# Expert weights at the end of a Fourier and expert kernel: six conversions moved, six loads placed elsewhere, fewer fill matmuls

## The chip, the cores and the metric

One core of one Trainium2 chip runs the whole program. The metric is device microseconds of one execution, and less is better. The core has five engines that run side by side, each in the order of its own queue: TensorE (PE, matmuls; its weight loads stand apart as PEld), VectorE (DVE), ScalarE (ACT), GpSimd (POOL) and SyncE (SP, which here only starts DMAs). POOL starts the gathers, whose row addresses come from memory.

## The reference, cut to what matters

```python
def _attn_ref(x, w_r, w_i, b_r, b_i):           # x: 8 x 2496 x 256
    X = np.fft.rfft(x, axis=1)
    Yr = Xr @ w_r - Xi @ w_i + b_r
    Yi = Xr @ w_i + Xi @ w_r + b_i
    Yr, Yi = soft_threshold(Yr, 0.01), soft_threshold(Yi, 0.01)
    return np.fft.irfft(Yr + 1j * Yi, n=2496, axis=1)

def _moe_ref(x, w_gate, w1, w2, capacity):      # x: 19968 x 256, 8 experts, capacity 80
    expert_idx, gate_w = argmax and its softmax of x @ w_gate
    for e in range(8):
        tok_idx = the 80 tokens of expert e with the largest gate_w
        h = np.maximum(x[tok_idx] @ w1[e], 0.0)           # w1[e]: 256 x 1024
        out[tok_idx] = gate_w[tok_idx, None] * (h @ w2[e])  # w2[e]: 1024 x 256
    return out                                  # all other rows are zero
```

## The kernel before, in words

The transform of length 2496 is split as 39 by 64 and done with matmuls, one batch after the other, in two halves each. The last step of the inverse transform is not done for all tokens. Its input lies in a DRAM tensor (`hd`), and for a chosen token 13 of its rows of 256 numbers are gathered and added with 13 weights (`wv`). The gate's values are formed for all tokens, and VectorE picks the best 80 of each expert by rounds of maximum and replace (`level1`, `level2`, `merge`, `choose`). This chooses 640 tokens. 128 of them are known early and gathered first (`ahead_`, `scaleA`, `columnsA`); the other 512 come as four groups of 128, numbered g = 0 to 3.

For each group `begin` and `feedY` issue on POOL a gather of ids (`tok`, L1124), then one of seven rows of `hd` (`hx`), one of the weights (`wv`) and one of the other six rows (`hx`). `position` adds the rows up on ACT, DVE and POOL (L1178, L1179, L1186, L1201, L1206, L1209, L1213). For groups 0 and 1 PE adds some of them with diagonal matrices that DVE makes (L1176, L1240). `columnsY` brings the sum onto PE, and ACT and DVE write it as an fp16 pair into `xT` (L1256, L1258). Then `experts` runs, expert by expert, `ffn1` (L1271, followed by L1273 on ACT and L1275 on DVE into `hp`) and `ffn2` (L1287, followed by L1290, L1291 or L1293 on ACT into `wt`), and `give` transposes finished groups (L1297), scales them (L1299) and scatters them into the output (L1300). Experts 0, 1 and part of 2 need group 0; expert 4 needs group 2; expert 6 needs group 3.

Expert weights arrive as fp32 and are used as a pair: a high half in fp16, made by ACT (a "conversion", L852, L855 or L858), and the rest in bf16, which is the fp32 weights less the high half (a "subtraction", on DVE at L860 or on POOL at L867). The text calls a quarter of an expert's weights (e, k, i): expert e, k = 0 for w1 and 1 for w2, half i. Each is 128 partitions by 1024 numbers, 512 KB. `prepW` makes these steps and `doW` traces the next of them. `slots["pairN"]` is the region of expert N: 4096 fp32 columns that hold, in this order, the high half of w1, the high half of w2, the rest of w1, the rest of w2, 1024 columns each. Before a quarter is converted it must be loaded into a free place: experts 4 to 6 are loaded into the region of expert 7 and into `stage`, and expert 7 into the region of expert 0, once that expert has been computed. Quarters (6,1,0) and (6,1,1) go into the first two pieces of expert 7's region, which (5,1,0) and (5,1,1) leave once DVE has subtracted them. The loads after these two are those of expert 7, and all six stand at L835 in SP's queue.

The order of each engine's queue is chosen at build time by a list scheduler that takes what is ready, in the order of tracing. `tc.issue_after(i)` puts what is traced in it behind instruction i on the same engine. `behind(key)` does so for an instruction that was noted in `ev`, and does nothing where the key is not there yet. In `ev`, ("A", "ra", e) and ("A", "rv", e) are L1273 and L1275 of expert e, ("A", "xa", g) and ("A", "xv", g) are L1256 and L1258 of group g. `exps` holds the exponentials of the gate (L785), `dev` and `d2s` evictions at L560 and L594, `sums` the three additions of `combine` on POOL (L579 to L581), `egs` the last gather of `ahead_`, `ffs` the copy of a flag on DVE (L1071), `hbs` and `hops` earlier DMAs on SP. `BUSY` counts matmuls without use that keep PE at work: the first number is that of L1768, the second that of L1226 after `columnsA`; four more of L1226 stand in the middle of group 0's columns.

Of the kernel before, what the change touches and what calls it, by code (L numbers as in the profile page):

```python
# [141 lines left out]
def fourier_mix_then_moe(ctx, tc, x, w_r, w_i, b_r, b_i, wg, w1, w2, t1, t2, vq, v3, v0, v1f, vt, sg, cst, cb, out):  # L142
# [276 lines left out]
    mids = []  # L419
    hbm = []  # L420
# [398 lines left out]
    def prepW(e, pool, name):  # L819
# [3 lines left out]
        def load(k, i):  # L823
            if (k, i) in got:
                return
            if e < E - 1:
                wt = stage2[0][:, i] if (e, k) == (2, 1) and stage2 else stage[(0, 1, 4, 5)[2 * k + i]] if e == 6 else stage.pop(0)
                if e != 6 and not ((e, k) == (2, 1) and stage2):
                    stage.append(wt)
            else:  # L830
                wt = slots["pair0"][:, 1024 * (2 * k + i):1024 * (2 * k + i) + 1024]
            w = w2[e].rearrange("(c p) d -> p c d", p=128)[:, 4 * i:4 * i + 4] if k else w1[e].rearrange("(c p) f -> p c f", p=128)[:, i:i + 1]
            if 4 * e + 2 * k + i >= 26 and after:
                with tc.issue_after(hbs[-1].ins if e == 6 else hops[-1].ins):
                    nc.sync.dma_start(wt.rearrange("p (c f) -> p c f", c=1 + 3 * k), w)  # L835
            else:
                (nc.sync.dma_start if e >= WS or stage2 else wdma)(wt.rearrange("p (c f) -> p c f", c=1 + 3 * k), w)
            got[k, i] = wt

        def step(k, i):  # L840
# [9 lines left out]
            if e == 7 and after:  # L850
                with behind(("A", "xa", 4) if k + i == 2 and ("A", "xa", 4) in ev else ("A", "ra", (3, 4)[k])):
                    nc.scalar.activation(wh[:, c:c + 1024], wt, AF.Copy)  # L852
            elif e >= HX and after:
                with behind(("A", "ra", k)) if e == 6 else tc.issue_after(dev[-1].ins):
                    nc.scalar.activation(wh[:, c:c + 1024], wt, AF.Copy)  # L855
            else:
                with tc.issue_after((exps[-2], exps[-2], d2s[0], exps[-1])[2 * k + i].ins) if after else ExitStack():
                    nc.scalar.activation(wh[:, c:c + 1024], wt, AF.Copy)  # L858
            if (e, k, i) in WV:
                sub = lambda: nc.vector.tensor_tensor(wl[:, c:c + 1024], wt, wh[:, c:c + 1024], op=ALU.subtract)  # L860
                with (behind(("A", 'xv', 3)) if e == 7 else behind(("A", "rv", k)) if e == 6 else tc.issue_after(ffs[-1].ins)) if after else tc.issue_after(sels[-1].ins):
                    sub()
            else:

                def sub():
                    with tc.issue_after((egs if (e, k, i) > (5, 0, 0) else sums)[-1].ins) if sums and e > 4 else ExitStack():
                        nc.gpsimd.tensor_tensor(wl[:, c:c + 1024], wt, wh[:, c:c + 1024], op=ALU.subtract)  # L867
                held.append(sub) if hold else sub()
# [293 lines left out]
    def position(S, nm, g, wv, hx):  # L1162
# [3 lines left out]
        if g in PEQ:  # L1166
# [12 lines left out]
            nc.scalar.activation(z, hx[1], AF.Copy, scale=w(1))  # L1179
# [49 lines left out]
    BUSY = (6, 12)  # L1229
# [89 lines left out]
    def ahead_():  # L1319
# [9 lines left out]
        with tc.issue_after(sums[-1].ins):  # L1329
            get(NL)  # L1330
            gather(hA[:, :1792], hd[0][:5 * 192], ct[:, NL, 1:2])
            gather(wv, vt, ct[:, NL, 2:3])
            egs.append(gather(hA[:, 1792:3328], hd[1][:5 * 192], ct[:, NL, 1:2]))
# [60 lines left out]
    def experts(S, n, gate, sid):  # L1394
# [27 lines left out]
        feedY(S)  # L1422
        feedY(S)
        first(0)
        if after:
            doW(2)
# [366 lines left out]
    with tc.high_priority():  # L1793
# [10 lines left out]
        S0.update(ct=sA["ct"])  # L1804
        sA.update(rest=S0["rest"])
    doW(len(wq) - 8)
    for q in wq[:4]:
        q[2]()
# [49 lines left out]
```

## Time and profile before

| what | us |
|---|---|
| three runs | 573.61, 1066.68, 579.05 |
| median of the three | 579.05 |
| the profiled execution's own time | 574.14 |
| its span, from the first to the last instruction | 572.4 |
| PE busy in it | 525.7 |

The profile's times count from the first instruction. The span covers the program's instructions, and 1.74 us of the profiled execution's own time lie around it. The transform takes the first 480 us, in which PE is nearly always busy. The work that the change touches lies after that: the picking of tokens to 508 us, the gathers and the experts from 512 to 564 us, and the last scatter, which starts at 564.49 us.

### The profile page before, as it was taken

The numbers are of one execution on the slowest core, as the hardware profiler recorded it, in microseconds if no ns is written. First come the engines' busy times: TensorE is split into PE (matmuls) and PEld (weight loads), VectorE is DVE, ScalarE is ACT, GpSimd is POOL, SyncE is SP. The second block draws the span as 40 slices with busy tenths as digits, with TensorE's granted clock in tenths as the row PEclk, the third lists the DMA queues.
The fourth block names the chain that finished last, engine by engine and source line by source line (L and its number), as shares of the span: only waits on it lengthen the run. The fifth ranks groups of instructions, "written<-read, shape, count | busy, mean of one in ns | idle before, by whom it ended". The sixth has DMA issues, their size and how long they took to land. (4 is left out here: it accounts for less than half of the span.)

```text
span 572.4 us, 12944 instructions
## 1 busy us (share of the span) xinstructions
PE 525.7 (92%) x5067; PEld 383.6 (67%) x5067; DVE 386.5 (68%) x741; ACT 328.1 (57%) x479; POOL 371.0 (65%) x295
## 2 busy tenths in 40 slices
PE   8869999999999999999999999979799998888993
PEld 3355676667677867786687768756676785556983
DVE  4423555666767676766766976784999958876950
ACT  2325768575756665675667565654564635641861
POOL 4105887686866786767678677576993166856661
PEclk9979999999999999999999999999999977989997
DMA  6898898987999798978996897889882778579800
GB/s 221 267 250 233 298 216 279 264 256 226 265 286 298 218 268 257 299 187 254 279 318 186 229 260 211 258 256 290 238 261 78 209 215 281 165 247 394 302 31 25
DMA packets 97224, 137.03 MB, mean 239 GB/s; under 512 B 26600, under 2 KB 77808, under 8 KB 95402
## 3 DMA queue, kind: packets, MB, share of 16 engines
q1 hardware_dynamic: 91115, 118.10, 71.1%
q0 software_dynamic: 2624, 11.45, 5.6%
q10 hardware_dynamic: 3418, 6.58, 3.6%
q8 instruction: 42, 0.69, 0.5%
q14 instruction: 25, 0.20, 0.1%
HBM read 70.82 MB, written 65.29 MB: 238 GB/s over the span
## 5 line engine op out<-in xcount | busy, mean ns | idle before, releaser
L450 PE MATMUL ps<-XT,WM 128*128 128x288 f16 (+4 forms) x1536 | 217.4, 298 | 7.5 <-DVE Gs L568 2.1
L450 PEld LDWEIGHTS <-WM 128*128 128x128 f16 x1536 | 149.4, 98 | 65.3 <-issue 7.5
L479 DVE SCALAR_TENSOR_TENSOR R<-ps,thr,tp 128x674 f32<-128x674 f32 (+1 forms) x56 | 48.6, 867 | 78.8 <-ACT tp L474 75.0
L497 POOL TENSOR_TENSOR YT<-R,YT 128x1408 f16<-128x1408 f32 (+1 forms) x28 | 73.5, 2623 | 31.9 <-ACT YT L496 30.2
L474 ACT ACTIVATE tp<-ps,thr 128x674 f32<-128x674 f32 (+1 forms) x56 | 43.6, 778 | 82.9 <-PE ps L450 78.0
L482 POOL TENSOR_TENSOR R<-R,sgs 128x576 f32<-128x576 f32 x28 | 36.5, 1302 | 75.0 <-DVE R L479 75.0
L301 POOL TENSOR_TENSOR xs<-xt,xs 117x1024 f16<-117x1024 f32 (+1 forms) x39 | 76.3, 1957 | 9.9 <-ACT xs L300 9.8
L386 PE MATMUL ps<-t2s,z 128*128 128x128 f16 x320 | 57.8, 222 | 9.0 <-DMA z<-zs 7.2
L337 DVE TENSOR_TENSOR zs<-ps,zs 128x1024 f16<-128x1024 f32 (+1 forms) x45 | 51.1, 1136 | 18.0 <-ACT zs L336 17.6
L392 DVE TENSOR_TENSOR XT<-ps,XT 128x640 f16<-128x640 f32 (+2 forms) x64 | 51.6, 815 | 15.6 <-ACT XT L391 15.0
L391 ACT ACTIVATE XT<-ps 128x640 f16<-128x640 f32 (+2 forms) x64 | 44.5, 701 | 24.2 <-PE ps L388 20.5
L387 PE MATMUL ps<-t2s,z 128*128 128x128 f16 x320 | 57.8, 222 | 0.0
L388 PE MATMUL ps<-t2s,z 128*128 128x128 f16 x320 | 57.8, 221 | 0.0
L315 PE MATMUL ps<-xs,t1s 117*128 117x512 f16 x213 | 52.5, 379 | 1.0 <-POOL xs L301 0.8
L336 ACT ACTIVATE zs<-ps 128x1024 f16<-128x1024 f32 (+1 forms) x45 | 43.0, 955 | 11.8 <-PE ps L315 6.9
L565 DVE TENSOR_TENSOR YO<-ps,YO 128x768 f16<-128x768 f32 (+1 forms) x50 | 45.3, 907 | 6.0 <-ACT YO L564 6.0
L616 PE MATMUL ps<-YO,vqs 128*128 128x512 f16 (+1 forms) x252 | 48.0, 330 | 1.5 <-DVE hs L623 1.5
L496 ACT ACTIVATE YT<-R 128x1408 f16<-128x1408 f32 (+1 forms) x28 | 35.5, 1267 | 21.2 <-POOL R L493 21.1
L553 PE MATMUL ps<-wgi,YT 128*128 128x144 f16 (+1 forms) x302 | 43.2, 228 | 3.3 <-DVE R L479 1.9
L554 PE MATMUL ps<-wgi,YT 128*128 128x136 f16 (+1 forms) x302 | 42.5, 225 | 0.0
L564 ACT ACTIVATE YO<-ps 128x768 f16<-128x768 f32 (+1 forms) x50 | 38.5, 775 | 3.9 <-PE ps L554 1.7
L616 PEld LDWEIGHTS <-vqs 128*128 128x128 f16 x252 | 24.3, 98 | 23.2 <-issue 2.5
(330 smaller groups left out, 978.6 us busy)
## 6 DMA issues: line engine op xcount, KB each, us to landing
out<-zero SPq DMA_DIRECT2D x48, 384.0 KB
z<-zs SPq DMA_DIRECT2D x35, 512.0 KB
hd<-hs SPq DMA_DIRECT2D x90, 192.0 KB
xt<-in_x SPq DMA_DIRECT2D x41, 312.0 KB
z<-z SPq DMA_DIRECT2D x14, 528.0 KB
pair<-in_moe_w SPq DMA_DIRECT2D x14, 512.0 KB
z<-z SPq DMA_DIRECT2D x14, 432.0 KB
wt<-in_moe_w ACTq DMA_DIRECT2D x10, 512.0 KB
```

The costliest lines, as they stand in the source:

```text
L301: nc.gpsimd.tensor_tensor(xs[:, 1, :ng], xt[:, j0:j0 + ng], xs[:, 0, :ng], op=ALU.subtract)
L315: nc.tensor.matmul(pt[:, 512 * j:512 * j + 512], t1s[:, t], xs[:, h, 2 * j:2 * j + 2], start=(i == 0), stop=(i == 2))
L337: evD.append(nc.vector.tensor_tensor(zs[:, :ng, 1, :], pv[:, :ng], zs[:, :ng, 0, :], op=ALU.subtract))
L386: nc.tensor.matmul(o, zz(0), t2s[:, cl, 0, :], start=True, stop=False)
L387: nc.tensor.matmul(o, zz(0), t2s[:, cl, 1, :], start=False, stop=False)
L388: nc.tensor.matmul(o, zz(1), t2s[:, cl, 0, :], start=False, stop=True)
L392: nc.vector.tensor_tensor(ov(1), pv, ov(0), op=ALU.subtract)
L450: nc.tensor.matmul(pt[:, o:o + e - a], WM[:, dh, m, wh, 128 * eh:128 * eh + 128], XT[:, dh, xh, c, a:e], start=(i == 0), stop=(i == len(te ...
L479: nc.vector.scalar_tensor_tensor(fv(Rf), pv, thr[:, eh, ri, 1:2], fv(t), op0=ALU.add, op1=ALU.min)
L497: nc.gpsimd.tensor_tensor(yv(1), rv, yv(0), op=ALU.subtract)
L565: dvs.append(nc.vector.tensor_tensor(yol, yy, yoh, op=ALU.subtract))
L616: nc.tensor.matmul(o, tab[:, v], yo(h), start=(i == 0), stop=(i == 2))
```

## The change

- Loads: quarters (6,1,0) and (6,1,1) go into the region of expert 0, into the places of w1's high half and w1's rest. (7,0,0) and (7,0,1) go into the fourth and the second piece of expert 7's own region, (7,1,0) and (7,1,1) into the places of w2's high half and rest in the region of expert 0. The six loads are put behind each other on SP. The first four are traced behind `ffn1` of expert 0; before, expert 6's were traced ahead of `experts` and expert 7's at expert 6.
- Conversions: (4,1,1) stands behind the eviction `d2s[0]` where it stood behind the last exponential; (5,0,0) behind the last exponential where it stood behind the last eviction; (6,0,0) and (6,0,1) behind L1179 of group 0 where they stood behind L1273 of expert 0; (7,0,0) and (7,0,1) behind L1256 of group 2 where they stood behind L1273 of expert 3.
- Subtractions: on POOL (5,0,0) stands behind nothing where it stood behind `combine`, and (5,0,1) behind the first gather of `ahead_` where it stood behind its last. On DVE (5,1,0) and (5,1,1) stand behind a new copy of one column that reads the ids of group 1, so it waits for that gather; (6,0,0) and (6,0,1) are traced ahead of `ffn1` of expert 0, so the key that held them behind L1275 is not there.
- Fill: `BUSY` is (4, 4) where it was (6, 12).

```diff
+    got1 = []
+    loads = []
...
-            if e < E - 1:
+            if after and e > 5 and e + k > 6:
+                wt = slots["pair7"][:, 3072 - 2048 * i:4096 - 2048 * i] if e + k == 7 and not k else slots["pair0"][:, 1024 * (e - 6) + 2048 * i:1024 * (e - 5) + 2048 * i]
+            elif e < E - 1:
...
-                wt = slots["pair0"][:, 1024 * (2 * k + i):1024 * (2 * k + i) + 1024]
+                wt = slots["pair0"][:, 1024 * (k + 2 * i):1024 * (k + 2 * i) + 1024]
...
             if 4 * e + 2 * k + i >= 26 and after:
-                with tc.issue_after(hbs[-1].ins if e == 6 else hops[-1].ins):
-                    nc.sync.dma_start(wt.rearrange("p (c f) -> p c f", c=1 + 3 * k), w)
+                with tc.issue_after(loads[-1].ins) if loads else ExitStack():
+                    i_ = nc.sync.dma_start(wt.rearrange("p (c f) -> p c f", c=1 + 3 * k), w)
+                loads.append(i_)
...
             if e == 7 and after:
-                with behind(("A", "xa", 4) if k + i == 2 and ("A", "xa", 4) in ev else ("A", "ra", (3, 4)[k])):
+                with behind(("A", "ra", 4) if k else ("A", "xa", 2)):
...
             elif e >= HX and after:
-                with behind(("A", "ra", k)) if e == 6 else tc.issue_after(dev[-1].ins):
+                with behind(("A", "ra", 1) if k else ("A", "az", 0)) if e == 6 else tc.issue_after((dev if k + i else exps)[-1].ins):
...
-                with tc.issue_after((exps[-2], exps[-2], d2s[0], exps[-1])[2 * k + i].ins) if after else ExitStack():
+                with tc.issue_after((exps[-2], exps[-2], d2s[0], d2s[0])[2 * k + i].ins) if after else ExitStack():
...
-                with (behind(("A", 'xv', 3)) if e == 7 else behind(("A", "rv", k)) if e == 6 else tc.issue_after(ffs[-1].ins)) if after else tc.issue_after(sels[-1].ins):
+                with (behind(("A", 'xv', 3)) if e == 7 else behind(("A", "rv", k)) if e == 6 else tc.issue_after(got1[-1].ins)) if after else tc.issue_after(sels[-1].ins):
...
-                    with tc.issue_after((egs if (e, k, i) > (5, 0, 0) else sums)[-1].ins) if sums and e > 4 else ExitStack():
+                    with tc.issue_after(egs[0 if e == 5 else -1].ins) if egs and after and (e, k, i) > (5, 0, 0) else ExitStack():
...
-            nc.scalar.activation(z, hx[1], AF.Copy, scale=w(1))
+            ev[nm, "az", g] = nc.scalar.activation(z, hx[1], AF.Copy, scale=w(1))
...
-    BUSY = (6, 12)
+    BUSY = (4, 4)
...
-            get(NL)
+            egs.append(get(NL))
...
         feedY(S)
+        if after:
+            doW(2)
         feedY(S)
         first(0)
         if after:
-            doW(2)
+            for q in wq[:4]:
+                q[2]()
...
+        with tc.issue_after(ffs[-1].ins):
+            got1.append(nc.vector.tensor_copy(sp.tile([128, 1], F32, name="t1"), ctA[:, 1, 0:1]))
...
-    for q in wq[:4]:
+    for q in wq[:2]:
         q[2]()
```

## Rows read from the trace of the kernel before

**Rows 1.** The head of the page: span and instructions.

```profile
span 572.4 us, 12944 instructions
```

**Rows 2.** The chain that ended last, in order of time: start us, us, what.

```profile
519.11 5.88 DMA wv<-in_vt,tok
...
526.81 2.61 PE pf L1271 x46
```

**Rows 3.** Windows: busy us of each engine (instructions), granted clock, DMA share, GB/s.

```profile
502.50:510.50 8.00, 6.00 (x22) 2.79 (x21) 6.02 (x23) 5.25 (x12) 4.05 (x3) 0.79 1.00 384
...
514.00:526.00 12.00, 9.86 (x67) 7.13 (x67) 5.46 (x14) 2.10 (x6) 8.93 (x9) 1.00 1.03 373
...
528.00:530.00 2.00, 2.00 (x25) 2.00 (x23) 1.97 (x6) 0.91 (x3) 1.14 (x2) 0.50 0.99 345
```

**Rows 4.** DMA queues and issues, 512 to 520 us; an issue's last number: us to landing.

```profile
q1 hardware_dynamic: 1045, 1.04, 47.7%
...
hx<-hd,tok POOLq DMA_INDIRECT x3, 6.9
```

**Rows 5.** DMA queues, 512 to 543 us: packets, MB, share of 16 engines.

```profile
q1 hardware_dynamic: 2400, 3.15, 30.9%
q0 software_dynamic: 1344, 6.85, 57.6%
```

**Rows 6.** Timeline of SP, weight loads: start us, us over all, what, how many.

```profile
513.02 1.50 SPq L835 DMA_DIRECT2D pair<-in_moe_w  x2
...
529.39 6.16 SPq L835 DMA_DIRECT2D pair<-in_moe_w  x4
```

**Rows 7.** Timeline of POOL: start us, us, what, count, idle before and its end.

```profile
486.17 2.14 POOL L867 TENSOR_TENSOR pair<-pair,pair 128x1024 bf16<-128x1024 f32 x1 [4.34 <-ACT pair L858]
...
502.50 2.15 POOL L867 TENSOR_TENSOR pair<-wt,pair 128x1024 bf16<-128x1024 f32 x1
...
512.52 1.28 POOL L1124 DMA_INDIRECT hx<-hd,tok  x1 [2.37 <-ACT pair L1338]
...
515.36 0.94 POOL L1124 DMA_INDIRECT hx<-hd,tok  x1 [0.31 <-issue]
...
543.81 4.23 POOL L867 TENSOR_TENSOR pair<-pair,pair 128x1024 bf16<-128x1024 f32 x2
```

**Rows 8.** Timeline of DVE.

```profile
502.71 2.00 DVE L1049 TENSOR_TENSOR Gs<-gh,t0b 8x48 f32<-8x48 f32 x1
...
505.37 0.20 DVE L1050 TENSOR_TENSOR Gs<-pfn,pfb 8x48 f32<-8x48 f32 x1
...
511.76 2.36 DVE L860 TENSOR_TENSOR pair<-pair,pair 128x1024 bf16<-128x1024 f32 x2
519.88 0.76 DVE L1176 TENSOR_TENSOR wt<-ident,wv 128x128 f32<-128x128 f32 x2 [5.76 <-issue]
...
530.88 2.36 DVE L860 TENSOR_TENSOR pair<-pair,pair 128x1024 bf16<-128x1024 f32 x2 [0.36 <-ACT pair L855]
```

**Rows 9.** Timeline of ACT.

```profile
506.41 5.51 ACT L1338 ACTIVATE pair<-pair 128x256 f32<-128x256 f32 x13 [0.88 <-DMA pair<-in_vt,tok]
...
525.07 0.51 ACT L1178 ACTIVATE y<-hx,wv 128x256 f32<-128x256 f32 x1 [4.01 <-DMA wv<-in_vt,tok]
...
536.37 2.01 ACT L855 ACTIVATE pair<-pair 128x1024 f16<-128x1024 f32 x2
...
542.68 2.00 ACT L852 ACTIVATE pair<-pair 128x1024 f16<-128x1024 f32 x2
...
549.04 1.99 ACT L852 ACTIVATE pair<-pair 128x1024 f16<-128x1024 f32 x2
```

**Rows 10.** Timeline of PE.

```profile
517.27 2.75 PE L1226 MATMUL pf<-pair 128*128 128x512 f16 x12
...
535.43 1.89 PE L1271 MATMUL pf<-xT,pair2a 128*128 128x80 f16 x48
...
545.27 0.44 PE L1297 MATMUL ps<-ident,wt 128*128 128x128 f32 x2 [1.00 <-ACT wt L1290]
```

## The prediction

> **What bounds the kernel now.** I read the page first, then the chain that ended last, then windows over the end of the span, and then the timelines of the five engines there. The change is traced behind the transform, so only the last 90 us of the span [rows 1] can move. The chain shows the reader a single transfer on the path to the first expert: the gather of group 1's weights `wv`, issued at 519.11 and 5.88 us on its way. After it come one step each on ACT and DVE and then PE's first `ffn1`, the bulk of which starts at 526.81 [rows 2]. The windows say why the transfer is slow: from 514 to 526 us the DMA engines are full (share 1.03, 373 GB/s) [rows 3]. The queue view says with what: to 520 us 1.04 MB are weights on SP's queue [rows 4], and from 512 to 543 us it is 3.15 MB of weights beside 6.85 MB of gathers [rows 5]. The weights of that early stretch are SP's two loads from 513.02; the other four start at 529.39 [rows 6]. So the stretch from 512 to 526 us waits for DMA, and two loads that nobody needs before 536.37 [rows 9] stand in it. From 526 us on PE is nearly always at work, with short waits for ACT, such as the 1.00 us at 545.27 [rows 10].
>
> **The early moves (480 to 512 us).** The subtraction of (4,1,1) goes into POOL's 4.34 us of idle time ahead of 486.17, and (5,0,0) takes its old place [rows 7]. Their conversions swap places on ACT in the same way. Price 0: POOL is idle there, and if that cover were gone 2.14 us would fall on `combine`. (5,0,1) leaves 502.50 [rows 7] for the place that (5,0,0) had. That frees DVE: L1049, an addition of 48 columns, took 2.00 us and ended with POOL's 2.15 us subtraction, where a like one, L1050, took 0.20 [rows 8]. So DVE's picking of tokens ends 1.8 us sooner. I let only 0.2 of it through, because what comes next is held by others: the DMA engines are full until 510.50 (share 1.00) [rows 3], the first `hx` gather must wait for the stores in that stretch, and ACT scales the early rows until 511.92 (506.41 and 5.51) [rows 9]. The gather starts at 512.52 [rows 7]. Bounds: 0 and -1.8; I take **-0.2**, nearer the rows that hold it. The Trainium skill, SBUF — State Buffer, section "Who interferes with whom", says that a VectorE instruction with two SBUF inputs and a GpSimd instruction that reads SBUF exclude each other for a whole instruction. The pair 502.50 and 502.71 agrees, and the same rule would spare the gathers from the DVE subtractions that the change puts beside them, since it takes descriptor writing to need another port. By the rule alone the +0.4 below would be 0 and the sum -2.5.
>
> **The two loads.** Without 1.04 MB ahead of or between the gathers, at 373 GB/s [rows 3, 4], group 0's second `hx` and group 1's `wv` land up to 1.04/0.373 = 2.8 us sooner. The least is 0, if POOL's issuing sets the pace: a gather's issue takes 0.94 us [rows 7], and four make a group. Issuing is a little faster than the DMA engines (a group is a quarter of 6.85 MB, 1.71 MB, 4.6 us at 373 GB/s, against some 5 us for four issues with the pauses of 0.31 between them, [rows 3, 5, 7]), so the two are close, and part of the gain must be lost to POOL. I take **-2.4**.
>
> **Quarters (6,0,0) and (6,0,1).** Their conversions (2 us by the like pair at 536.37) fall into ACT's wait of 4.01 us ahead of 525.07 [rows 9]: price 0, and if `wv` landed at once they would cost up to 2. Their DVE subtractions (2.36 us at 530.88 [rows 8]) now stand among group 0's and group 1's additions. DVE does the same work in all, so what they cost early comes back at 530.88. What does not come back is a delay of the gathers: beside L860 at 511.76 [rows 8] the `hx` issue took 1.28, and 0.94 at 515.36 [rows 7], so 0.34 for each that meets one. Bounds 0 and +2.36; I take **+0.4**, one such meeting. The new copy of ids holds (5,1,0) and (5,1,1) behind the ids' landing. DVE is idle for 5.76 us behind them, ahead of 519.88 [rows 8], so the price is 0, and up to 2 if group 0's rows came that early.
>
> **Fill.** Twelve matmuls at 517.27 take 2.75 us [rows 10]; four take 0.9. PE waits for `wv` of group 0 behind them, so alone this is worth 0; once that lands sooner, the twelve would have held group 0's columns, which is why both edits belong together. Two fewer of L1768 also go to PE idle time. What can be lost is the clock, priced below as a rival.
>
> **Loads of (6,1,0) and (6,1,1) later.** They now wait for the end of `ffn1` of expert 0, as two of expert 7's did at 529.39 [rows 6]. With the 2.2 gained so far that is about 527.2. The trace gives no landing for SP's loads, so I take the nearest, 6.9 us for `hx` in a full stretch [rows 4]: 534.1. Their conversions start at 536.37 [rows 9], less 2.2, at 534.2. So the cover is just used up: behind the conversions on ACT stand L1273 of the next experts, for which `ffn2` waits. Bounds 0 and +2; I take **+0.3**.
>
> **Conversions of (7,0,0) and (7,0,1).** At 542.68 they hold ACT for 2.00 us [rows 9], and L1290 and group 2's L1256 stand behind them; PE waits 1.00 for L1290 [rows 10]. Behind L1256 of group 2 they hold neither. Bounds 0 and -1.00; I take **-0.9**.
>
> **A new wait.** (7,1,0) is converted into the second piece of expert 7's region, from which (7,0,1) is now subtracted by POOL. The conversions of (7,1,*) start at 549.04 [rows 9] and POOL's two subtractions run from 543.81 for 4.23 us [rows 7], to 548.04. That is 1.0 us of margin. With the first pair's conversions 2 us later relative to the rest, the margin is -1. Behind this ACT instruction stand L1290 of expert 3 and L1273 of expert 5, and PE waits for both. Bounds 0 (the scheduler puts other work ahead) and +2.1 (one more subtraction); I take **+0.7**.
>
> **The sum.** -0.2 - 2.4 + 0.4 + 0.3 - 0.9 + 0.7 = -2.1. The profiled execution took 574.14 us, 572.4 of it span [rows 1], so 572.0. That execution is 4.91 below the median shown, 579.05, and 0.53 above the lowest run. I forecast on its footing and let the range reach up for the other.
>
> **The rivals.** *No gain*: POOL's issuing sets the gathers' pace, or PE's clock takes the gain. In the profile the clock is granted at 0.50 (1.2 GHz) from 528 to 530 us, after PE's short stretches of work to 526 [rows 3], and 46 matmuls took 2.61 us where 48 took 1.89 at full clock [rows 2, 10], some 0.8 us for each such stretch. With eight fewer matmuls the clock could fall twice, +1.6, and with the two loads worth 1.2 rather than 2.4 the sum is -2.1 + 1.6 + 1.2 = +0.7: 574.8. The Trainium skill, TensorE: Matmul & The Clock Gate, section "What's actually happening", takes the slow clock as the default that activity lifts. By that rule less fill is a loss, and this rival is where it would show. *Slower*: ACT's wait at the conversion of (7,1,0). If the two loads bring nothing (0 for -2.4), that wait costs one whole subtraction, 2.1 for the 0.7: -2.1 + 2.4 + 1.4 = +1.7: 575.8. It decides once POOL ends (7,0,1) later than ACT reaches the conversion by more than the 1.0 that the earlier edit saves. *More gain*: the loads bring 2.8, ACT's wait goes whole, no new wait comes, and the slow clock at 528 vanishes (0.8): -0.2 - 2.8 - 1.0 - 0.8 = -4.8: 569.3. *The change does not do what it says*: the scheduler takes the old order on ACT and DVE, and only the loads' places change, which is the first rival's time.
>
> **How the numbers follow.** Forecast 572.0 with chance 0.45, its own range 570 to 574; no gain 0.22; slower 0.18; more gain 0.12; 0.03 for what none of these covers. The low end goes below the third rival by 1.8, to 567.5. The high end takes the slower rival with most of the 4.91 by which the median lies above the profiled execution: 575.8 + 4.2 = 580. Faster or slower by over 2% is 11.5 us, about what a measurement of this kernel can tell from no change, and no term or sum of terms reaches it: faster 0.04, slower 0.04, within 0.92.
>
> **What would show it.** Right: `wv` of group 1 lands near 522.6 and PE's first `ffn1` runs at about 524.5; L1049 takes 0.2; no 1.00 wait at L1297 behind L1290. Wrong: conversions L855 of (6,1,*) that wait for a DMA, a conversion L852 that waits for POOL's L867 with PE idle behind it, or a granted clock of 0.50 over more than the 3 us of now.

## The result and the profile after

The median of 20 executions after the change is 578.43 us, that of 20 before it 575.45 us. The ratio is 1.0062, with an interval of 1.0037 to 1.0087: some 3.5 us slower, where 2.1 us faster was forecast. (All ratios are taken from the fast executions of both kernels alone, so they are not quite the ratios of the medians.) A second measurement of the same kernel in a later session (`after_anchor` below) gave the same median, 578.45, beside 577.83 for before: 1.0015 [0.9982, 1.0047]. The two together put the cost at about 0.4%, 2.2 us. The first interval says 2.1 to 5.0 us slower, the second 1.0 faster to 2.7 slower. By 2% this is no change; the sign of the sum was wrong all the same, and that is what had to be explained.

The profiled execution after took 581.63 us, high among its own 20 (576.35 to 586.23). So its rows show what can happen, and prices are taken from several kernels' traces. The head of its page, for [rows 1]:

```profile
span 579.8 us, 12925 instructions
```

The chain that ended last (start us, us, what), for [rows 2]:

```profile
506.79 9.35 DMA pair<-hd,tok
...
516.16 1.31 ACT pair L1343 x3
...
521.38 5.22 DMA hx<-hd,tok
...
532.96 1.80 PE pf L1276 x46
534.77 10.69 DMA pair<-in_moe_w
545.48 1.06 ACT pair L860
546.57 1.23 DVE pair L865
547.79 0.40 DVE yp L1218
548.19 0.40 DVE hp L1280
548.60 0.04 issue
548.64 1.76 PE pf L1276 x24
```

Two transfers stand here that the chain before did not show. One is the gather of the early rows (`pair<-hd,tok`), for whose rows ACT, POOL and so the first `hx` gather wait. It is not new: the chain before is followed back only to 514.11, and before, too, the first `hx` gather waited 2.37 us for ACT's work on these rows [rows 7]. The other is new: a weight load of 10.69 us, for which ACT, DVE and PE wait in turn. It is the one that the prediction had costed with 6.9 us. Timelines of SP, ACT and PE (idle before, and its end, in brackets) for [rows 6, 9, 10]:

```profile
534.77 8.16 SPq L839 DMA_DIRECT2D pair<-in_moe_w  x6
...
525.54 1.99 ACT L860 ACTIVATE pair<-pair 128x1024 f16<-128x1024 f32 x2
530.12 0.51 ACT L1183 ACTIVATE y<-hx,wv 128x256 f32<-128x256 f32 x1 [2.59 <-DMA wv<-in_vt,tok]
...
545.48 1.06 ACT L860 ACTIVATE pair<-pair 128x1024 f16<-128x1024 f32 x1 [4.44 <-DMA pair<-in_moe_w]
...
548.64 1.76 PE L1276 MATMUL pf<-xT,pair 128*128 128x80 f16 x24 [3.28 <-DVE hp L1280]
```

The conversion of (6,1,0) at 545.48 waits 4.44 us for its load, and PE then waits 3.28. The conversions of (6,0,*) at 525.54 do fit into ACT's wait for `wv`. Timelines of POOL and DVE, for [rows 7, 8]:

```profile
498.85 1.06 POOL L1129 DMA_INDIRECT tok<-cid,posA  x1 [0.17 <-DVE ps L922]
499.93 2.14 POOL L872 TENSOR_TENSOR pair<-wt,pair 128x1024 bf16<-128x1024 f32 x1
504.25 0.97 POOL L1129 DMA_INDIRECT pair<-hd,tok  x1 [2.18 <-issue]
...
517.82 2.00 POOL L1129 DMA_INDIRECT hx<-hd,tok  x1 [6.22 <-ACT pair L1343]
...
529.44 1.61 POOL L1129 DMA_INDIRECT hx<-hd,tok  x1 [0.30 <-issue]
531.36 1.30 POOL L1129 DMA_INDIRECT wv<-in_vt,tok  x1 [0.30 <-issue]
...
505.94 0.20 DVE L1054 TENSOR_TENSOR Gs<-gh,t0b 8x48 f32<-8x48 f32 x1
```

The addition that had taken 2.00 us takes 0.20, as forecast. But the gather of the early rows at 504.25 comes 5.40 us after the gather of their ids at 498.85. The same two gathers before:

```profile
495.63 1.06 POOL L1124 DMA_INDIRECT tok<-cid,posA  x1 [0.17 <-DVE ps L917]
496.71 2.14 POOL L867 TENSOR_TENSOR pair<-wt,pair 128x1024 bf16<-128x1024 f32 x1
499.01 0.97 POOL L1124 DMA_INDIRECT pair<-hd,tok  x1 [0.16 <-issue]
```

There it was 3.38. Windows of after (busy us of PE, PEld, DVE, ACT, POOL; clock, DMA share, GB/s), for [rows 3]:

```profile
514.00:526.00 12.00, 9.65 (x60) 8.26 (x58) 4.01 (x8) 5.86 (x15) 6.65 (x6) 0.86 0.59 200
526.00:538.00 12.00, 9.79 (x125) 8.84 (x126) 10.77 (x25) 4.56 (x12) 9.50 (x9) 0.86 0.88 294
538.00:548.00 10.00, 6.62 (x180) 6.39 (x178) 5.25 (x14) 5.56 (x16) 3.52 (x5) 1.00 1.02 380
```

From 514 to 526 us the DMA engines are no longer full (share 0.59; 1.03 before), in part because the gathers start at 517.82 only. From 538 to 548 us, where the late loads run beside the last groups' gathers, they are full (1.02), and PE is busy for 6.62 of 10 us.

### The profile page after: what moved, and what is told of

Read it like the earlier page. It is cut to its first block, busy times and chain, and to the rows that moved or that the text cites. A ratio compares the mean times of both kernels' runs of the same rounds, so it can differ in the third digit from the quotient of the medians.

```text
span 579.8 us, 12925 instructions
## 1 busy us (share of the span) xinstructions
PE 529.1 (91%) x5057; PEld 389.5 (67%) x5057; DVE 385.0 (66%) x742; ACT 328.5 (57%) x479; POOL 372.7 (64%) x295
## 4 chain that ended last, share of the span: by engine, by line
PE 48%; DVE 15%; DMA 13%; POOL 7%; ACT 7%; issue 7%; SPq 2%; POOLq 0%; ACTq 0%; DVEq 0%
PE ps L452 21%; PE ps L315 6%; PE ps L618 4%; DMA wt<-in_moe_w 3%; DMA xt<-in_x 3%; DVE R L481 2%; DMA pair<-in_moe_w 2%; PE ps L555 2%; PE ps L556 2%; ACT tp L476 2%; DMA z<-zs 2%; DMA pair<-hd,tok 2%; POOL R L484 2%; PE ps L386 1%; PE ps L646 1%
## 5 line engine op out<-in xcount | busy, mean ns | idle before, releaser
L386 PE MATMUL ps<-t2s,z 128*128 128x128 f16 x320 | 59.1, 224 | 8.4 <-DMA z<-zs 7.2
L337 DVE TENSOR_TENSOR zs<-ps,zs 128x1024 f16<-128x1024 f32 (+1 forms) x45 | 51.1, 1135 | 17.2 <-ACT zs L336 16.9
L387 PE MATMUL ps<-t2s,z 128*128 128x128 f16 x320 | 59.1, 224 | 0.0
L388 PE MATMUL ps<-t2s,z 128*128 128x128 f16 x320 | 59.1, 224 | 0.0
L555 PE MATMUL ps<-wgi,YT 128*128 128x144 f16 (+1 forms) x302 | 44.6, 232 | 2.7 <-DVE R L481 1.4
L556 PE MATMUL ps<-wgi,YT 128*128 128x136 f16 (+1 forms) x302 | 43.8, 229 | 0.0
```

The lines of the kernel that those rows point to most:

```text
L386: nc.tensor.matmul(o, zz(0), t2s[:, cl, 0, :], start=True, stop=False)
L387: nc.tensor.matmul(o, zz(0), t2s[:, cl, 1, :], start=False, stop=False)
L388: nc.tensor.matmul(o, zz(1), t2s[:, cl, 0, :], start=False, stop=True)
L555: nc.tensor.matmul(pt[:, off:off + w], yt(0), wgi[:, eh, 0:w], start=True, stop=False)
L556: nc.tensor.matmul(pt[:, off:off + w - w % 128 // 2], yt(1), wgi[:, eh, 0:w - w % 128 // 2], start=False, stop=True)
```

## Experiments

All ratios are to the kernel before on the same chip, from 12 or 13 executions and 35 of before. Theory A: the loss comes from the loads of (6,1,0) and (6,1,1), which are late and come in short pieces. Rival B: it comes from the front, up to the first gathers.

### The loads

`no_loads` is the change with all six loads in their old places and order.

```diff
-            if after and e > 5 and e + k > 6:
+            if False:
...
-                with tc.issue_after(loads[-1].ins) if loads else ExitStack():
+                with tc.issue_after(hbs[-1].ins if e == 6 else hops[-1].ins):
...
```

> The changed kernel with all six loads back in their old places and order, everything else as changed. Theory A (the two loads of expert 6's w2 come too late: in the changed kernel's trace ACT stands 4.44 us ahead of the conversion at 545.48 for a DMA, and PE then 3.28 us for DVE): that wait goes, ACT's conversions of (6,1,*) find their data, and the time falls by about 4 us from the changed kernel's +3.5, to a ratio of 0.997 to 1.000. Theory B (the loss is made at the front, by the DVE subtractions of (6,0,*) and (5,1,*) among the gathers and group 0's additions, and the loads' new places even help): the loads come back among the gathers, and the ratio stays at 1.006 or rises to 1.010.

Measured: 578.17 us, 1.0000 [0.9975, 1.0026]. That is the upper end of what theory A had, and the value that rival B had lies outside the interval. But in its trace the gather of the early rows is late as well (4.89 us behind its ids), so that alone does not make a kernel slower than before.

`loads_only` is the kernel before with the new places and order of the loads, and nothing else.

> The kernel before with the six loads in their new places and order, nothing else changed. Theory A: wv of group 1 lands 1 to 2 us sooner, but ACT waits 3 us or more for the load of (6,1,0) at its conversion, and the ratio is 1.003 to 1.007, most of the whole change. Theory B: the ratio is 0.995 to 0.999, since only the help is left.

Measured: 580.31 us, 1.0033 [1.0002, 1.0064]. In its executions some 2.1 us lie around the span, 1.8 in those of before, so a small part of the loss is not in the rows. Its timelines of ACT, of PE and of POOL:

```profile
525.60 0.51 ACT L1183 ACTIVATE y<-hx,wv 128x256 f32<-128x256 f32 x1 [3.94 <-DMA wv<-in_vt,tok]
...
528.83 0.44 ACT L1261 ACTIVATE xT<-ps 128x192 f16<-128x192 f32 x2 [2.33 <-remote]
...
539.56 1.08 ACT L860 ACTIVATE pair<-pair 128x1024 f16<-128x1024 f32 x1
...
543.53 1.06 ACT L860 ACTIVATE pair<-pair 128x1024 f16<-128x1024 f32 x1 [1.70 <-SPq L1820]
...
529.72 3.22 PE L1276 MATMUL pf<-xT,pair 128*128 128x80 f16 x46 [0.28 <-DVE xT L1263]
...
513.68 1.97 POOL L1129 DMA_INDIRECT hx<-hd,tok  x1 [1.68 <-ACT pair L1343]
```

A wait for a late load is there, as theory A had it, but it is smaller and elsewhere: the first quarter, at 539.56, is converted 6.0 us after SP starts the loads at 533.56 and waits for nothing, and ACT waits 1.70 us for the second, where 3 or more were expected. The ratio lies at the low end of what was expected. These rows also price the gain: ACT uses group 1's `wv` 11.92 us after the first `hx` gather starts (525.60 less 513.68), where it was 12.55 before (525.07 less 512.52, [rows 9, 7]) and is 12.30 after (530.12 less 517.82). That is 0.63 or 0.25 us, not 2.4. And nothing of it reaches PE here: ACT's next step waits 2.33 us for something that the profile does not name, and the bulk of the first `ffn1` on PE starts 16.04 us after the first `hx` gather (529.72 less 513.68), where it was 14.29 before (526.81 less 512.52) and is 15.14 after (532.96 less 517.82). Over the traces that distance is 14.3 to 16.2 us in the seven with the old loads, mean 15.35, and 14.3 to 16.4 in ten of the eleven with the new, mean 15.41 (19.9 in the eleventh, `no_early_pe_p2`). What ACT waits for there stays open.

`w1_rows` is the change with the late loads of (6,1,*) reading expert 6's `w1`, whose pieces are 4 KB long where those of `w2` are 1 KB. So expert 6's second product is made with other weights, of the same size and number. In the choice of `w`, `r1` stands for `k` in the same way.

```diff
+            r1 = k and not (e == 6 and after)
...
-                    i_ = nc.sync.dma_start(wt.rearrange("p (c f) -> p c f", c=1 + 3 * k), w)
+                    i_ = nc.sync.dma_start(wt.rearrange("p (c f) -> p c f", c=4 if r1 else 1), w)
```

> The changed kernel, but the two loads of (6,1,*) read rows of expert 6's w1 (128 pieces of 4 KB) in place of w2's (512 pieces of 1 KB): the same 512 KB at the same place in the queue, so expert 6's w2 is not the reference's. Theory A in its narrower form (piece by piece the DMA engines take turns between the gathers' 7 KB rows and the loads' 1 KB rows, so a load of small rows gets the small share while gathers are in flight): (6,1,0) lands after 5 to 7 us where it took 10.7, ACT's wait shrinks from 4.4 to under 2 us, and the ratio falls to 1.001 to 1.003. If only the late issue counts and the rows' size does not: landing stays near 10 us and the ratio at 1.006.

Measured: 577.47 us, 1.0005 [0.9974, 1.0035]. Its conversions of (6,1,*) stand at 537.92 and 540.88, the first of them 5.67 us after SP starts the loads at 532.25 and without a wait; the second waits 0.38 us for its load. This fits theory A, but its profile also lacks the late gather at the front, so it does not settle A alone.

### The early moves

`early_only` is the kernel before with the moves of (4,1,1), (5,0,0) and (5,0,1) alone.

```diff
-                with behind(("A", "ra", k)) if e == 6 else tc.issue_after(dev[-1].ins):
+                with behind(("A", "ra", k)) if e == 6 else tc.issue_after((dev if k + i else exps)[-1].ins):
...
-                with tc.issue_after((exps[-2], exps[-2], d2s[0], exps[-1])[2 * k + i].ins) if after else ExitStack():
+                with tc.issue_after((exps[-2], exps[-2], d2s[0], d2s[0])[2 * k + i].ins) if after else ExitStack():
...
-                    with tc.issue_after((egs if (e, k, i) > (5, 0, 0) else sums)[-1].ins) if sums and e > 4 else ExitStack():
+                    with tc.issue_after(egs[0 if e == 5 else -1].ins) if egs and after and (e, k, i) > (5, 0, 0) else ExitStack():
```

> The kernel before with the early moves alone: (4,1,1), (5,0,0) and (5,0,1). Both theories: the addition of 48 columns on DVE takes 0.2 us instead of 2.0, tokens are picked 1.8 us sooner, and little of it gets past the stores and gathers that fill the DMA engines: ratio 0.998 to 1.000. If the first gather of rows hung on DVE after all, 0.997.

Measured: 579.79 us, 1.0032 [1.0001, 1.0063]. A miss: moves priced at nothing cost 1.9 us by themselves, with an interval that begins just above nothing. In its trace the gather of the early rows comes 5.02 us after that of their ids. So theory A is not enough, and the next four runs take the early moves out.

`no_early` is the whole change without them, `rest_only` without them and without the loads; `conv7_only` is the kernel before with one edit:

```diff
-                with behind(("A", "xa", 4) if k + i == 2 and ("A", "xa", 4) in ev else ("A", "ra", (3, 4)[k])):
+                with behind(("A", "ra", 4) if k else ("A", "xa", 2)):
```

> The whole change without the early moves of (4,1,1), (5,0,0) and (5,0,1). Theory E: 1.002 to 1.004, that is 0.3% less than the 1.0062 of the whole change, and the gathers of the early rows follow their ids after 3.4 us as before, not after 5.4. Rival (early moves cost nothing): 1.005 to 1.007.

Measured: 576.03 us, 0.9981 [0.9953, 1.0009], lower than theory E. Its timeline of POOL and of ACT:

```profile
495.59 1.06 POOL L1129 DMA_INDIRECT tok<-cid,posA  x1 [0.17 <-DVE ps L922]
498.97 0.97 POOL L1129 DMA_INDIRECT pair<-hd,tok  x1 [0.16 <-issue]
...
537.13 1.06 ACT L860 ACTIVATE pair<-pair 128x1024 f16<-128x1024 f32 x1
...
540.67 1.06 ACT L860 ACTIVATE pair<-pair 128x1024 f16<-128x1024 f32 x1 [0.97 <-SPq L1821]
```

The gap is 3.38 us again, and the late loads, issued at 530.72, cost ACT 0.97 instead of 4.44.

> The kernel before with four of the six edits: the copy of ids that holds (5,1,*), the subtractions and conversions of (6,0,*), the conversions of (7,0,*) and the fill; the early moves and the loads stay as before. Theory E (the early moves cost about 0.3%, as they did alone, and the loads the rest of the loss): 0.995 to 0.999, since all but the loads together were 1.000. Rival (the early moves cost nothing and 1.0032 was the spread of the measurement): 0.999 to 1.001, the same as with the early moves.

Measured: 576.24 us, 1.0000 [0.9977, 1.0023]: the rival's value.

> The kernel before with one edit: conversions of (7,0,0) and (7,0,1) stand behind group 2's columns on ACT. The prediction gives this -0.9 us and, since these places are loaded early as before and no late load stands behind them, no new wait worth more than 0.7: a ratio of 0.9975 to 0.9995. Rival (the wait of 1.00 us at the finished group comes back elsewhere, since ACT has the same work): 1.000 or above.

Measured: 575.05 us, 0.9969 [0.9942, 0.9996]. This is the one kernel of the sixteen that is faster than before by more than its interval, and only just, so it may be in part a lucky draw among many. Its 1.8 us is also twice the 0.76 that its trace accounts for. PE's wait of 1.00 us at the finished group [rows 10] is down to 0.24:

```profile
545.83 0.44 PE L1302 MATMUL ps<-ident,wt 128*128 128x128 f32 x2 [0.24 <-ACT wt L1295]
```

`swap6_no_early` also lacks the early moves, and loads expert 6's `w2` early and its `w1`, with the long pieces, late; nothing is left out of the computation.

```diff
+            q = 1 - k if e == 6 and after else k
-            if after and e > 5 and e + k > 6:
+            if after and e > 5 and e + q > 6:
...
-            if 4 * e + 2 * k + i >= 26 and after:
+            if 4 * e + 2 * q + i >= 26 and after:
...
```

> The whole change without the early moves, and with expert 6's two halves in each other's parts: its w2 is loaded early and converted first, its w1, whose pieces are 4 KB long instead of 1 KB, is loaded late into the freed region of expert 0. Theory A (short pieces make the late loads slow): 0.996 to 0.999 if the early moves cost 0.3%, 0.999 to 1.001 if they cost nothing; the late loads take about 5 us from issue and ACT waits for them 0.5 us or less. Rival (it is the late place in the order, not the length of the pieces, and reading the wrong tensor made the earlier run look good): 1.002 or above, with ACT waiting over 2 us for these loads.

Measured: 575.50 us, 0.9984 [0.9953, 1.0014], with no wait of ACT for these loads, as theory A has it; but `no_early` with short pieces is as good.

### The meeting at the ids

What holds the gather of the early rows? DMA packets by queue (packets, MB, share of 16 engines) in the 2.25 us from the start of the ids' gather, first after:

```profile
q1 hardware_dynamic: 41, 0.13, 22.2%
q8 instruction: 1, 0.02, 4.9%
q0 software_dynamic: 30, 0.00, 1.8%
```

and before:

```profile
q1 hardware_dynamic: 11, 0.03, 6.1%
q0 software_dynamic: 32, 0.00, 5.9%
```

The gather of the ids has 32 packets. Before, all of them have passed and no instruction packet is there yet. After, one packet of kind instruction, 16 KB, is on its way, and two packets of ids are not through; the last ends 3.64 us after the gather's start. Theory P: the instruction packet sits ahead of the last ids on their DMA engine. (The profile does not say on which engine a packet runs, so this can be judged by times alone.) The same rows hold a rival: 41 packets of q1, SP's queue, pass in this time where 11 did, so SP's stores also come earlier. Over a whole execution there are 42 instruction packets, 0.69 MB, and PE with its weight loads executes 10,114 of the 12,925 instructions, so I took them for PE's. Four kernels shift them, by more or fewer matmuls without use ahead of a 7 us wait of PE at 25 us:

```diff
-    for _ in range(34):
+    for _ in range(30):
         pin(nc.tensor.matmul(pt[:, 0:512], warm[:, 0:128], warm, start=True, stop=True))
```

> The whole change with 30 instead of 34 of the matmuls without use that stand ahead of PE's 7 us wait at 25 us. PE's later work is unchanged, but each of its 42 instruction packets of 16 KB is asked for four matmuls later in the program. In the traces of the whole change such a packet starts 1.8 us after the gather of the early rows' ids is issued and holds the last ids until 3.6 us; without the early moves it starts at 2.2 us, behind the ids, which are there at 2.2. Theory P (that meeting is what the early moves cost): the packet starts at 3 us, the next gather follows the ids' gather after 3.4 us, not 5.4, and the ratio falls from 1.0062 to 0.997 to 1.001. Rival (the early moves cost through something else): the ratio stays at 1.004 to 1.008.

Measured: 576.95 us, 0.9992 [0.9960, 1.0025], and the packet comes 3.06 us behind the ids' gather. As theory P has it:

```profile
497.31 1.06 POOL L1129 DMA_INDIRECT tok<-cid,posA  x1 [0.16 <-DVE ps L922]
500.69 0.97 POOL L1129 DMA_INDIRECT pair<-hd,tok  x1 [0.16 <-issue]
```

> The whole change with 42 instead of 34 of the same matmuls, so that the packet comes some 2.7 us earlier in PE's work and is through ahead of the ids. Theory P: the gap between the two gathers is 3.4 us and the ratio 0.997 to 1.001. Rival: the gap stays above 4.8 us, or it falls and the ratio stays at 1.004 to 1.008.

Measured: 578.38 us, 1.0011 [0.9980, 1.0041]. The packet did not come earlier (1.79 us behind the ids' gather) and the gap is 4.54: the shift missed, and the ratio says nothing for either.

> The change without the early moves, with 36 instead of 34 of the same matmuls: the packet should start 0.6 us earlier, at about 1.6 us after the ids' gather, and so meet the ids without any early move. Theory P: the gap between the gathers is 4.8 to 5.4 us and the ratio rises from 0.998 to 1.003 to 1.007. Rival: the gap stays at 3.4, or it rises and the ratio stays at 0.998.

Measured: 577.74 us, 0.9998 [0.9968, 1.0028]. The packet came at 2.34 and the gap stayed at 3.39: no meeting was made.

> The kernel before with 36 instead of 34 of the same matmuls and nothing else. Theory P: the packet meets the ids, the gap between the gathers rises from 3.4 to about 5 us, and the ratio is 1.002 to 1.004, as with the early moves alone (1.0032). Rival: 0.999 to 1.001.

Measured: 576.75 us, 0.9983 [0.9954, 1.0011]. Packet at 2.29, gap 3.38: no meeting here either. It is also a measure of the noise, since hardly anything is changed in it.

So the number of matmuls ahead does not place the packet by itself. But the stores, the rival, do not place the gap by themselves either. Three kernels have the early moves and yet the short gap: `after_pe_m4`, `w1_rows` and `swap6` (below). In these three the stores pass at the same time and in the same number as in the change: 35 to 39 packets in the 2.25 us, the first 1.77 or 1.78 us behind the start of the ids' gather. In five traces with the long gap it is 33 to 40, from 1.78 to 1.80 us on. What differs is the instruction packet, which starts 3.06 to 3.18 us behind the start in the three and 1.7 to 1.8 in the five. In these five, moreover, the last two packets of ids start within 0.02 us of the instruction packet's end. The next candidate was ACT: before, four conversions stand ahead of the eviction L650 for which PE stops; with (5,0,0) moved up there are three, and the eviction starts 0.23 us ahead of the ids' gather (498.62, 498.85) where it started 0.20 behind it (495.83, 495.63).

`after_anchor` is the change again, unchanged; `before_conv5` is the kernel before with the first of the three edits of `early_only`, and `after_conv5_back` the change without it.

> The whole change again, beside the next three on the same chip. If 1.0062 is what it costs: 1.003 to 1.009.

Measured: 578.45 us, 1.0015 [0.9982, 1.0047], below what was expected; gap 4.94.

> The whole change, with the conversion of (5,0,0) back behind the last eviction, so that ACT has three conversions in a row again ahead of the last PSUM evictions and PE stops for them. Theory P (this conversion is what brings the instruction packet to 1.8 us behind the ids' gather, onto the ids): the packet starts at 2.2 us or later, the gap between the gathers is 3.4 us, and the ratio lies 0.5% or more under that of the whole change on the same chip. Rival (the early moves cost by something else, such as POOL's subtractions): gap and ratio as in the whole change.

Measured: 579.78 us, 1.0033 [1.0009, 1.0056], gap 4.90: theory P's step through ACT is refuted as the only way. The run is not clean, since POOL's subtraction of (5,0,0) fell behind `combine` with it and the ids' gather starts 2.1 us later than in the change, counted from the gate's last exponential.

> The kernel before with one edit: the conversion of (5,0,0) behind the last exponential. Theory P: the packet starts at 1.8 us behind the ids' gather, the gap is 4.8 to 5.4 us, and the ratio is 1.002 to 1.004. Rival: the gap stays at 3.4 us and the ratio at 0.999 to 1.001.

Measured: 579.13 us, 1.0021 [0.9985, 1.0057]. One edit makes the gap long, as expected:

```profile
498.39 1.06 POOL L1129 DMA_INDIRECT tok<-cid,posA  x1 [0.17 <-DVE tk L923]
503.42 0.97 POOL L1129 DMA_INDIRECT pair<-hd,tok  x1 [1.81 <-issue]
```

> The whole change with expert 6's halves in each other's parts, so that the late loads have pieces of 4 KB. If the late loads and the meeting at the ids cost about 0.3% each: 0.3% under the whole change on the same chip, 1.002 to 1.004. If the loads cost only where the gathers they meet are late, and all of it then: 0.999 to 1.001. If long pieces change nothing: as the whole change.

Measured: 577.59 us, 0.9999 [0.9971, 1.0026], 0.16% under the change beside it. By chance the packet came at 3.18 in its profile, with a gap of 3.38, so it too differs in both suspects.

### What the sixteen say together

The meeting: in the ten traces with any early move the gap is 4.5 to 5.4 us seven times and 3.38 three times (`w1_rows`, `after_pe_m4`, `swap6`). In the eight without one (before among them) it is 3.38 or 3.39 each time. Wherever it is long, the instruction packet starts 1.4 to 2.0 us behind the ids' gather; wherever it is short, 2.2 us or more. In two of the seven the fit is loose: the last ids start 0.9 us after the packet's end in `before_conv5` and 0.3 to 0.5 after it in `after_conv5_back`, among more packets of stores. The delay is passed on: from the ids' gather to the first `hx` gather it is 15.8 to 16.9 us with the short gap and 17.6 to 19.0 with the long one (`after_conv5_back`, whose ids are late, has 16.3). That is a link in time and order, seen in 18 traces; what places the packet was not found. The link to the measured time is weaker: the seven runs with the long gap measure 1.0025 on the mean (`no_loads` among them 1.0000), the three with early moves and the short gap 0.9999, and the seven other runs, without early moves, 0.9993. But this grouping was made afterwards, and each gap is known from one profiled execution only.

The ratios: with the early moves less without, the four pairs give +0.58% (mean of the two measurements of the change, less `no_early`), 0 (`no_loads`, `rest_only`), +0.32% (`early_only`) and +0.15% (`swap6`, `swap6_no_early`): mean +0.26%, 1.5 us. Late loads with short pieces less the old ones: +0.39% (the change, `no_loads`), +0.33% (`loads_only`), -0.19% (`no_early`, `rest_only`): mean +0.18%, 1.0 us. With long pieces they give -0.01% (`swap6`, `no_loads`) and -0.16% (the two without early moves). Each ratio is known to some 0.3%, so the first mean stands clear of 0 by little and the second does not. The pairs leave out the three kernels with shifted matmuls; the mean of `after_pe_m4` and `after_pe_p8`, less `no_early_pe_p2`, is about 0, and counted as a fifth pair it brings the first mean to +0.2%. Whether the two costs add or call each other up stays open: without either the kernel loses nothing (`rest_only`), and the change's two measurements, 0.4% on the mean, cannot be told from 0.33% and 0.32% with one of them alone.

## Why the prediction was wrong, step by step

**The early moves: forecast -0.2, bounds 0 and -1.8; about +1.5.** This is the step that failed first, and it failed in its sign; the +1.5 itself is known to about 1.2 us. The part on DVE was right (0.20 at L1054), and so was the remark that the next work is held by others. But one of these others is the gather of the early rows, and with the moves it comes later in seven traces of ten. The prediction had read a chain that is followed back only to 514.11 and saw "a single transfer" on it; it took ACT's work on the early rows as fixed and did not ask when their gather would come. The price of 0 looked at POOL's idle time and not at what a conversion taken from ACT's row does to the evictions, to PE and to the DMA engines behind it. A bound above nothing was missing. By what way the moves bring the instruction packet ahead of the ids is not shown.

**The two loads: -2.4; at most some -0.6, and nothing that reaches PE.** This term failed too: the transfer gains, and the path does not. The transfer of group 1's `wv` did get faster, from 5.96 us between issue and use (519.11 to 525.07, [rows 2, 9]) to 4.66 in `loads_only` and 5.00 after. But the first `hx` issue took 1.97 and 2.00 where it took 1.28 [rows 7], and `wv` was issued 0.7 us later for it, so counted from the first `hx` gather the use comes only 0.63 and 0.25 us sooner. And of that nothing is seen at PE's first `ffn1`, as shown under `loads_only`: the next wait takes it. And the loads had used time that the gathers leave empty. Windows of 2 us from the first `hx` gather on, in `loads_only`:

```profile
513.70:515.70 2.00, 2.00 (x20) 2.00 (x20) 2.00 (x2) 0.30 (x1) 1.95 (x1) 1.00 0.00 0
515.70:517.70 2.00, 2.00 (x21) 2.00 (x20) 0.27 (x1) 0.00 (x0) 1.44 (x2) 1.00 0.65 133
517.70:519.70 2.00, 2.00 (x18) 1.70 (x17) 0.00 (x0) 0.00 (x0) 1.39 (x3) 1.00 0.98 379
```

and before:

```profile
512.50:514.50 2.00, 2.00 (x21) 2.00 (x20) 1.62 (x2) 0.00 (x0) 1.67 (x2) 1.00 0.39 13
514.50:516.50 2.00, 2.00 (x21) 2.00 (x20) 0.00 (x0) 0.00 (x0) 1.50 (x2) 1.00 0.88 321
```

In the first 4 us the gathers alone move 0.27 MB in `loads_only` (0.25 to 0.47 in the other traces) and gathers with loads 0.67 before, so up to 0.4 of the 1.04 MB went where nothing else did. The prediction had a mean over the full 12 us [rows 3] and divided by it.

**(6,0,*) and the meetings with DVE: +0.4; about 1.0 in the issues, not followed to the end.** The first `hx` issue is no part of it: it meets the subtractions of (5,1,*) in every kernel, and it took 1.28 before, 1.65 in `before_pe_p2`, 1.73 in `conv7_only` and 2.00 after, so its size varies without the change. The new meetings, with (6,0,*), are the issues at 529.44 and 531.36, which took 1.61 and 1.30 where 0.94 is usual: 0.67 and 0.36 more. Whether they reach the end is not shown. The prediction named a rule of the Trainium skill, SBUF — State Buffer, section "Who interferes with whom", by which the gathers would be spared. The traces do not bear this out: over the 18, 136 issues of gathers beside no DVE instruction with two inputs took 0.94 to 1.06 us, and 51 beside a 128x1024 subtraction 0.93 to 3.50, median 1.30. No run isolates it.

**Loads of (6,1,*) later: +0.3, bounds 0 and +2; about 1.5 of wait.** The risk was named, and the row that would show it ("conversions of (6,1,*) that wait for a DMA") came. The 6.9 us was a fair middle: over the seven traces of kernels with short late pieces and earlier conversions of (6,0,*), the first conversion comes 6.2 to 8.3 us after SP's issue, and 10.7 in the profiled execution of the change. ACT's waits for the two quarters in them are 4.44, 1.57, 1.34, 1.24, 0.97, 0.77 and 0, 1.5 on the mean. So the wait was larger than the term by 1.2, and by 4 in the execution shown. ACT's wait is not time one for one, though: `no_early` waits 0.97 and measures 0.9981. What the loads meet are the last groups' gathers. Queues from 539 to 543.5 us after:

```profile
q0 software_dynamic: 255, 1.38, 78.5%
q1 hardware_dynamic: 298, 0.30, 20.5%
```

Nearly as many packets of loads as of gathers pass, but with a fifth of the bytes: 1.0 KB each against 5.4. The Trainium skill, DMA: Bandwidth & Descriptors, section "Queues, rings and completion order", says that an engine takes turns between queues packet by packet; the nearly equal counts fit that. The packets also show what the length of the pieces does. The two late loads are 1024 packets of 1 KB, or 256 of 4 KB. As many as that had passed on SP's queue 9.0 to 11.7 us after its first issue in the seven traces with short pieces whose late loads meet gathers (11.67 after; 4.7 in `no_early_pe_p2`, where they meet none), and after 4.8 to 6.8 us in the three with long pieces.

**(7,0,*) conversions: -0.9.** Right in the wait: 1.00 became 0.24 in `conv7_only`, and the ratio there is 0.9969.

**The new wait at (7,1,0): +0.7.** It did not come; the conversions stand at 556.91 after, with other work put ahead of them, so the slower rival by that mechanism is out.

**Fill and clock.** The granted clock of 0.86 over two stretches of 12 us after stands against one such stretch before; but `no_early`, with the same fill, has 0.97 and 0.86 there, and `conv7_only`, with the old fill, 0.82 over 14 us and is the fastest. No price can be read from this. Something remains here that no run settles: over the executions that the ratios rest on, the mean granted clock lies 0.002 to 0.009 under that of before on the same chip in each of the eleven runs above with the new fill (mean 0.004), and from 0.004 under to 0.003 above it in the five with the old (mean 0.000). `no_early` and `swap6_no_early`, which are among the eleven, are not slower than before, so this alone does not explain the loss; but no run changes the fill alone, and it stays an open rival.

**The sum again**, now from runs where there are any: early moves +1.5, the new loads +1.0 (their gain at the front within it), the conversions of (7,0,*) -0.8 by the trace. That is +1.7, against about +2.2 measured. The first two are known to 1.2 us or worse, `no_early` beside `rest_only` has the loads at -0.19%, and taking `conv7_only`'s own time for the third would give less, so that the sum comes near may be chance.

The forecast of no change by 2% and the range held; the likeliest case did not. That the range held is luck in part. Its upper end is the slower rival, 575.8, and 4.2 us for a median that lay 4.91 above the profiled execution in three runs. Over 20 executions it lies 1.3 above (575.45 less 574.14), and 575.8 + 1.3 = 577.1 is under the 578.43 measured. And the loss came by other ways than the one that this rival names.

## What to carry to other kernels

Taking bytes out of a full stretch pays only for the part that others could have used: look at the first microseconds after each issue, where a gather moves nothing yet. Then follow the gain to the engine that bounds the kernel, since the next wait may take it, as here. A load that is put off is slower by what it meets and by the shortness of its pieces, so late loads should have the longest ones; the packets show this here, the measured times do not clear the noise. And a move into idle time of one engine needs a bound above nothing, for what its old neighbours then do sooner: here an eviction 0.4 us earlier went with some 1.5 us lost elsewhere, a link that was argued from the order of things and not shown.

## What was not expected of the hardware

- A gather of rows moves its first data only some 2 us after POOL starts it: the DMA share is 0.00 for 2.0 us and 0.65 in the next 2 (`loads_only`), and full after 4. In the eleven traces with the late loads the first data of the first `hx` gather come 2.2 to 2.7 us after its start, and 3.3 to 4.3 in the six where the two loads are issued beside it.
- A load of instructions, one packet of 16 KB that takes 1.0 to 1.8 us, goes with 1.1 to 2.0 us more until the gather that needs the ids can start, though only two of the 32 packets of ids were still to come when it began to hold them (the change's queues above). In five traces these two start within 0.02 us of its end.
- POOL's issue of a gather takes 0.94 to 1.06 us, and beside a DVE subtraction of 128x1024 numbers up to 3.50 us (`no_loads`), median 1.30, over the 18 traces.
- Two loads of 512 KB in pieces of 1 KB need 9.0 to 11.7 us beside gathers with 5 to 7 KB per packet, and 4.8 to 6.8 us in pieces of 4 KB, by the number of packets that have passed.
